# An mLSTM cell and a multiplicative feed-forward block on one core: first steps without products of zero states, other unread products, w_out fetched later

## The chip, the core and the metric

The kernel runs on one core of one Trainium2 chip. The metric is the device time in microseconds (us), from the start to the end of one execution. Lower is better. The kernel before has a median of 429.15 us over 3 runs (426.0 to 430.21).

## What is computed

The first half is an mLSTM cell over 4 sequences of 768 steps with 8 heads of 40 elements. Its output, seen as 3072 tokens of 320 elements, is the input of a feed-forward block in which two products are multiplied element by element:

```python
# per step t; C (40x40) and n (40) start at zero, m is a running maximum
m_new = np.maximum(f_gate[:, :, t] + m, i_gate[:, :, t])
f_stab = np.exp(f_gate[:, :, t] + m - m_new)
i_stab = np.exp(i_gate[:, :, t] - m_new)
C = f_stab * C + i_stab * np.einsum('bhd,bhe->bhde', vt, kt)
n = f_stab * n + i_stab * kt
h_tilde = np.einsum('bhde,bhe->bhd', C, qt)
denom = np.maximum(np.abs(np.einsum('bhd,bhd->bh', n, qt)), 1.0)
y[:, :, t] = sigmoid(o_gate) * h_tilde / denom
...
a = x @ w1          # 3072x320 @ 320x1024
b = x @ w2
h = a * b @ w3      # 1024x1024
return h @ w_out    # 1024x320
```

All data is float32.

## The kernel before

**Tiling.** The sequences are cut into 6 stretches of 128 steps, each of two chunks of 64. A unit is one stretch of one sequence with all heads: 24 units, n = 0 to 23, and unit n belongs to sequence n % 4. The main loop (L812) runs 32 steps s. Step s does the inner part of unit s (scores of q and k, and the new contribution to the state) and the output of unit s-1. The feed-forward products of finished units are put into the same steps, so that TensorE has work while the other engines prepare the next unit. w3 is multiplied into w_out on the chip (`w3_mm`, L256), so that only the product of both is used at the end.

**What a step's cell consists of (`quarter_work`, L335).** For unit s-1: 16 products `ph` of the masked weights pw with v, and 16 products `pi` of q with the state that the unit began with. For unit s: 16 products `ss` of k with q, and 16 products `pc` of k with weighted v, which VectorE adds to the state. Each of these is 64 wide at most, so four of them sit in the four quarters of the TensorE array, in the order of `quarters` (L104). In `pi`, hip is the half of the array's rows and x the chunk, that is the half of its columns; chunk x = 0 reads the state before the unit and x = 1 the state between the two chunks:

```python
for p in range(NP):
    for hip, x in quarters:            # quarters = ((0, 0), (1, 1), (0, 1), (1, 0))
        mm(pi[halves[x], hip, p, :], qT[heads[hip], p, halves[x]], before[x][heads[hip], p, :])
```

In the first four units the state before the unit is all zeros. The results of `ss` and `pc` are in the PSUM tile `cell0`, those of `pi` (and of `ph` from unit 2 on) in `cell1`.

**Order.** TensorE's instructions stay in the order in which they are written: `mm` (L91) and `transpose` (L94) chain each one to the one before (`in_order`, L84). Every `mm` of float32 appears in the trace as two weight loads (PEld) and two matmuls (PE), a transpose as one of each. On the other engines the order is the scheduler's; `keep_order` and `issue_after` hold parts of it. The queue of SyncE (SP) issues nearly all loads, in the order of the code.

**Products that nobody reads.** `warm(n)` (L97) multiplies the identity by itself n times into a spare PSUM bank. It is called with 8 at L579, before the first transposes, and with 5 at L893, in the function `between` of step 2, between `x_trans(0)` and `x_trans(1)`. `x_trans(n)` (L473) transposes the output y of unit n, as three transposes into a tile px, for the feed-forward block; it needs y of that unit from VectorE (L440).

**Step 2.** `between` (L884) scales and converts weight pieces, transposes y of units 0 and 1, turns unit 2's q and k (`turn`, tiles pt), and does the first feed-forward products (`up`, tiles pa and pb, and `up_rest` with the rest of the weights, wr).

**Weights.** The weights come as raw 8-byte words: `fetch` (L208) issues the DMA into one of the raw buffers, `scale_next` (L230) scales it on ScalarE (L188, L192), and `convert` (L234) makes float32 of it on VectorE (L196, L197). After the 10 pieces of w1, w2 and their rest come 8 of w_out and 16 of w3. `n_cvt[s]` (L806) pieces are converted at the end of step s. At the end of a step the loop at L968 fetches until `fetched` is 4 ahead of `converted`.

**PSUM.** Four banks (`ps_m`) serve the tiles of `mps` (L77) in turn; a bank can be written when its earlier tile has been read.

Of the kernel before, what the change touches and what calls it, by code (L numbers as in the profile page):

```python
# [16 lines left out]
def kernel(  # L17
# [26 lines left out]
    nc = tc.nc  # L44

    B, H, S, D = q.shape
    L = 64
    P = 128
# [3 lines left out]
    NP = H // 2  # L52
    DP = 64
    D1 = D + 1
# [20 lines left out]
    cell = [ps_c.tile([P, 2, 512], FP, name=f"cell{i}", tag=f"cell{i}") for i in range(2)]  # L75

    def mps(shape, name):  # L77
        pool = banks.pop(0)
        banks.append(pool)
        return pool.tile(shape, FP, name=name, tag="m")  # L80
# [3 lines left out]
    def in_order(ins):  # L84

        if last:
            tc.add_manual_dep(ins.ins, last.pop().name, mybir.DependencyInfo(
                mybir.DependencyClass.NoSync, mybir.DependencyReason.DATA), reason="in_order")
        last.append(ins.ins)

    def mm(out, lhsT, rhs, start=True, stop=True):  # L91
        in_order(nc.tensor.matmul(out, lhsT=lhsT, rhs=rhs, start=start, stop=stop))  # L92
# [1 line left out]
    def transpose(out, in_, n=P):  # L94
        in_order(nc.tensor.transpose(out, in_, ident[0:n, 0:n]))  # L95

    def warm(n):  # L97
        bank = mps([P, P], "fill")
        for _ in range(n):
            mm(bank, ident, ident)  # L100

    halves = [slice(0, L), slice(L, P)]
    heads = [slice(0, D), slice(DP, DP + D)]
    quarters = ((0, 0), (1, 1), (0, 1), (1, 0))  # L104
# [4 lines left out]
    N_DIAG = 2  # L109
# [5 lines left out]
    ident = const.tile([P, P], FP, name="ident")  # L115
# [179 lines left out]
    def weights(n):  # L295
        c, b = divmod(n, B)
        src = weights_tile(n) if n else spread(n)
        pw = weights_tile(n)
        for h in range(H):
            nc.scalar.activation(out=pw[:, h, :], in_=src[:, h, :], func=AF.Exp, bias=aT[:, c, b * H + h:b * H + h + 1])  # L300
# [7 lines left out]
    def turn(n):  # L308


        if n >= N_DVE:
            for src, dst, name in zip(turned_in[n % 2], (kT_t, qT_t), ("kT", "qT")):
                dst[n] = sb.tile([128, NP, P], FP, name=name, tag=name)
                done = nc.vector.transpose(out=dst[n].rearrange("i p (r f) -> i p f r", f=4),
                                           in_=src[:, 32:TB].rearrange("i (p f d) -> i p f d", p=NP, f=4)[:, :, :, 0:32])
            return done
        for src, dst, name in ((kbuf[n % NB], kT_t, "kT"), (qbuf[n % NBQ], qT_t, "qT")):
            pt = mps([128, NP, P], "pt")
            for p in range(NP):
                transpose(pt[:, p, :], src[:, 2 * p:2 * p + 2, :].rearrange("p a b -> p (a b)"))  # L320
            dst[n] = sb.tile([128, NP, P], FP, name=name, tag=name)
            nc.scalar.copy(out=dst[n], in_=pt)
# [12 lines left out]
    def quarter_work(s, rest, between, late):  # L335


        rest()

        def part(j, c0, n):  # L340
            return cell[j][:, :, c0:c0 + NP * n].rearrange("p x (n d) -> p x n d", d=n)

        ss, pc, pi = part(0, 0, L), part(0, NP * L, D1), part(1, 0, D1)
        ph = [cell[1][:, x, NP * D1:2 * NP * D1].rearrange("p (h d) -> p h d", d=D1) for x in range(2)]
        n = s - 1
        if 0 <= n < NU:
            pw, vt, qT = u_t.pop(n), vbuf[n % NBV], qT_t.pop(n)
            before = before_t.pop(n)

            if n < N_DIAG:  # L350
                ph = mps([P, H, D1], "ph")
                for hq in range(H):
                    for r in halves:
                        mm(ph[r, hq, :], pw[r, hq, :], vt[r, hq, :])
            for hd in range(H // 2 if n >= N_DIAG else 0):
                for x, e in quarters:
                    hq = hd if x == e else hd + H // 2
                    mm(ph[x][halves[e], hd, :], pw[halves[x], hq, :], vt[halves[x], hq, :])
            for p in range(NP):
                for hip, x in quarters:  # L360
                    mm(pi[halves[x], hip, p, :], qT[heads[hip], p, halves[x]], before[x][heads[hip], p, :])
        den = None
        if 0 <= s - 1 < NU:
            den = outputs(s - 1, pi, ph)
            den()
            if between:
                for _ in range(3):
                    den()
                den = None
                between()  # L370
            if late:
                late()
        n, first_read = s, None
        if n < NU:
            c, b = divmod(n, B)
            kt, vw = kbuf[n % NB], vw_t.pop(n)
            ends = range(2 if c < NT2 - 1 else 1)
            first, second, after = state[b]
            before_t[n] = first, second
            state[b] = after, second, first  # L380
            kT, qT, pw = kT_t.pop(n), qT_t[n], u_t[n]
            for p in range(NP):
                for hip, x in quarters:
                    mm(ss[halves[x], hip, p, :], kT[heads[hip], p, halves[x]], qT[heads[hip], p, halves[x]])
            M = D if n else L
            for p in range(NP):
                for x, e in quarters:
                    if x in ends:
                        mm(pc[e * L:e * L + M, x, p, :], kt[halves[x], 2 * p + e, 0:M], vw[halves[x], 2 * p + e, :])
        if n < NU:  # L390
            pv = pw.rearrange("p (n two) t -> p two n t", two=2)
            first_read = nc.vector.tensor_tensor(out=pv, in0=ss, in1=pv, op=OP.mult)
        with tc.issue_after(first_read.ins) if first_read else nullcontext():
            if den:
                den()
            if n < NU:

                if c:
                    nc.vector.tensor_tensor(out=second, in0=pc[:, 0], in1=second, op=OP.add)  # L399
                else:  # L400
                    nc.vector.tensor_copy(out=second, in_=pc[:, 0])
                if len(ends) > 1:
                    decayed(after, second, n, 1)
            if late:
                late()
            if den:
                den()
            if n < NU and len(ends) > 1:
                nc.vector.tensor_tensor(out=after, in0=pc[:, 1], in1=after, op=OP.add)
            if den:  # L410
                done = den()
        return done if den else first_read
# [104 lines left out]
    fetch("w12", 4, 0)  # L517

    nc.vector.memset(on, 1.0)
    nc.vector.memset(on.rearrange("p (c t) -> p c t", t=L)[:, :, 0:1], 0.0)  # L520
    nc.vector.memset(M[third[0], 0:1], 0.0)
    make_identity(nc, ident)
# [49 lines left out]
    def gate_cols(src, dst, copy):  # L572
        pg = mps([P, GC // 2, GR, BH], "pg")
        for c in range(GC // 2):
            transpose(pg[:, c].rearrange("p g r -> p (g r)"), src[:, c * P:(c + 1) * P], RG)
        for c in range(GC // 2):
            copy(out=dst.rearrange("p (g c) r -> p c g r", g=GR)[:, c], in_=pg[:, c])

    warm(8)  # L579
    turn(0)  # L580
    gate_cols(a, aT, nc.scalar.copy)
    nc.scalar.activation(out=dec, in_=U3[:, :, L - 1], func=AF.Exp)
    scale_next(True)
# [4 lines left out]
    for i, r in enumerate(third):  # L588
        nc.gpsimd.tensor_tensor(out=pick[r, :, i, :], in0=pair[r].to_broadcast([BH, B * NP, GC]), op=OP.mult,
                        in1=dec[r].unsqueeze(1).to_broadcast([BH, B * NP, GC]))  # L590
    weights(0)
    gate_cols(w, wT, nc.scalar.copy)
    weighted(0)
    masks(0)
# [208 lines left out]
    n_out = [0] * 27 + [1, 0, 1, 0, 3]  # L803
    w12 = [("w12", i, part) for part in range(2) for i in range(2 * KF + 1)]
    todo = w12[5:] + [("wo", i, 0) for i in range(FO)] + [("w3", ko, part) for ko in range(FO) for part in range(2)]
    n_cvt = [0, 0, 2, 0, 1, 2, 3, 3, 3] + [2] * 6  # L806
    n_fetch = [5, 5, 10]
    pinned, ahead = 32, 9
    behind = ExitStack()
    turned, converted, fetched = 0, 2, 5  # L810

    for s in range(len(n_up)):  # L812
# [4 lines left out]
        if s < 3:  # L817
# [6 lines left out]
            if s == 2:  # L824
                for _ in range(2):
                    fetch(*todo.pop(0))
                fetched = 10
# [56 lines left out]
        def between():  # L884
            twice(1)
            weighted(2)
            rows_of_u(3)
            for _ in range(3):
                scale_next()
            for n in range(2):  # L890
                x_trans(n)
                if n == 0:
                    warm(5)  # L893
            for _ in range(3):
                convert()
            turn(2)
            block = up(*now[0])
            weighted(3)
            weights(3)
            masks(3)  # L900
            out_gate(2)
            convert()
            up_rest(*block)
# [32 lines left out]
        if s in (2, 3):  # L936
            turned, converted = 2, converted + (4 if s == 2 else 2)
# [27 lines left out]
                scale_next()  # L965
        if N_DVE <= s + 2 < NU:
            load_turned(s + 2)
        while todo and fetched < (n_fetch[s] if s < len(n_fetch) else converted + 4):  # L968
            fetch(*todo.pop(0))
            fetched += 1  # L970
        if s + 1 == pinned:
# [32 lines left out]
```

## Time and profile before

| what | value |
|---|---|
| the profiled execution | 430.57 us |
| its span, first to last instruction | 428.5 us |
| three runs | 426.0, 429.15, 430.21 us |
| TensorE matmul busy / weight load busy | 410.7 us (96%) / 336.6 us (79%) |
| VectorE, ScalarE, GpSimd busy | 312.2, 149.8, 154.7 us |
| mean granted TensorE clock | 0.992 |
| moved by DMA | 51.15 MB, 135211 packets, mean 119 GB/s |
| instruction queue of TensorE (q8) | 42 packets, 0.69 MB |

A time in the views is counted from the start of the span. In a timeline a row gives the start, the length, the engine, the line of code, the operation, what it writes and reads, the shape (`64*64 64x41` is a weight tile of 64 rows and 64 columns and a result of 64 x 41) and the number of instructions. In brackets stands the idle time of the engine before it and what ended it; "issue" means that the engine waited for nothing that the profile shows. Most of `mm`'s calls have L92 as their line, so groups are told apart by their tiles.

### The profile page before, as it was taken

The numbers are of one execution on the slowest core, as the hardware profiler recorded it, in microseconds if no ns is written. First come the engines' busy times: TensorE is split into PE (matmuls) and PEld (weight loads), VectorE is DVE, ScalarE is ACT, GpSimd is POOL, SyncE is SP. The second block draws the span as 40 slices with busy tenths as digits, with TensorE's granted clock in tenths as the row PEclk, the third lists the DMA queues.
The fourth block names the chain that finished last, engine by engine and source line by source line (L and its number), as shares of the span: only waits on it lengthen the run. The fifth ranks groups of instructions, "written<-read, shape, count | busy, mean of one in ns | idle before, by whom it ended". The sixth has DMA issues, their size and how long they took to land.

```text
span 428.5 us, 13080 instructions
## 1 busy us (share of the span) xinstructions
PE 410.7 (96%) x5353; PEld 336.6 (79%) x5353; DVE 312.2 (73%) x634; ACT 149.8 (35%) x404; POOL 154.7 (36%) x211
## 2 busy tenths in 40 slices
PE   7789979999999999999999999999999999999996
PEld 5678768888788688788777677787778778888896
DVE  6768874788949769779726866586877699575972
ACT  4866843576725514521333313132311110210000
POOL 4530431333203113203307833645462577542200
PEclk9999969999999999999999999999999999999999
DMA  8999888398897866886335566666421120000001
GB/s 188 219 177 231 202 141 141 93 198 189 210 188 142 186 173 116 187 161 133 73 95 112 139 130 148 138 139 112 100 43 37 35 38 2 31 2 31 2 32 61
DMA packets 135211, 51.15 MB, mean 119 GB/s; under 512 B 109360, under 2 KB 126960, under 8 KB 135152
## 3 DMA queue, kind: packets, MB, share of 16 engines
q1 hardware_dynamic: 131552, 46.29, 53.2%
q10 hardware_dynamic: 3600, 4.03, 2.7%
q8 instruction: 42, 0.69, 0.7%
q14 instruction: 17, 0.14, 0.1%
HBM read 44.50 MB, written 5.80 MB: 117 GB/s over the span
## 4 chain that ended last, share of the span: by engine, by line
PE 69%; issue 9%; SPq 7%; DMA 5%; DVE 4%; POOL 3%; ACT 0%; DVEq 0%; POOLq 0%; ACTq 0%
PE cell L92 19%; PE pa L92 19%; PE pb L92 12%; PE o L92 8%; PE wp L92 6%; PE p L92 3%; SPq L136 3%; DMA raw<-in_moe_w_dram 3%; SPq L181 2%; DVE w3T L658 1%; PE pt L95 1%; POOL pw L305 1%; POOL raw L651 1%; PE px L95 1%; SPq L150 1%
## 5 line engine op out<-in xcount | busy, mean ns | idle before, releaser
L332 POOL TENSOR_TENSOR state<-state,decay 128x164 f32<-128x164 f32 x40 | 20.2, 504 | 154.7 <-DVE state L399 127.1
L92 PE MATMUL pa<-xT,w 128*128 128x256 f32 x240 | 62.0, 390 | 0.0
L92 PEld LDWEIGHTS pa<-xT,w 128*128 128x128 f32 x240 | 45.5, 195 | 6.8
L300 ACT ACTIVATE pw<-pw,aT 128x64 f32<-128x64 f32 x184 | 46.4, 337 | 3.2 <-ACT o_sb L733 1.9
L92 PE MATMUL pb<-xT,w 128*128 128x256 f32 x192 | 45.6, 380 | 0.7 <-DVE w L197 0.7
L92 PEld LDWEIGHTS pb<-xT,w 128*128 128x128 f32 x192 | 36.5, 191 | 6.1 <-DVE w L197 1.1
L721 POOL TENSOR_TENSOR ab<-ab,a_sb 128x512 f32<-128x512 f32 x22 | 29.4, 1357 | 32.0 <-DVE ab L676 32.0
L703 POOL TENSOR_TENSOR wo<-wo 128x512 f32<-128x512 f32 x22 | 27.5, 1270 | 31.5 <-DVE wo L678 31.5
L92 PE MATMUL pa<-xT,wr 64*64 64x256 f32 x384 | 37.0, 386 | 0.7 <-DVE wr L197 0.7
L92 PE MATMUL wp<-wo,w3T 128*128 128x320 f32 x128 | 35.9, 433 | 1.5 <-issue 1.1
L305 POOL TENSOR_SCALAR_AFFINE_SELECT pw<-pw 64x512 f32<-64x512 f32 x48 | 36.0, 750 | 3.1 <-ACT pw L300 1.4
L92 PE MATMUL pb<-xT,wr 64*64 64x256 f32 x384 | 36.4, 380 | 0.0
L92 PE MATMUL cell<-w3o,ab 128*128 128x320 f32 x128 | 35.4, 432 | 0.0
L630 ACT ACTIVATE a_sb<-pa 128x512 f32<-128x512 f32 x24 | 14.3, 596 | 60.3 <-PE pb L92 60.3
L631 DVE TENSOR_TENSOR ab<-pb,a_sb 128x512 f32<-128x512 f32 x24 | 16.4, 688 | 25.4 <-ACT a_sb L630 25.1
L92 PEld LDWEIGHTS wp<-wo,w3T 128*128 128x128 f32 x128 | 23.8, 190 | 10.9 <-issue 1.3
L92 PEld LDWEIGHTS cell<-w3o,ab 128*128 128x128 f32 x128 | 24.3, 190 | 9.5
L92 PEld LDWEIGHTS pa<-xT,wr 64*64 64x64 f32 x384 | 18.9, 132 | 15.6 <-issue 8.8
L425 DVE TENSOR_TENSOR h<-cell,h 64x164 f32<-64x164 f32 x88 | 28.7, 326 | 1.7
L678 DVE SCALAR_TENSOR_TENSOR a_sb<-pa,wo 128x512 f32<-128x512 f32 x12 | 8.3, 689 | 28.1 <-PE pa L92 28.1
L92 PE MATMUL po<-w3o,ab 128*128 128x320 f32 x96 | 26.4, 433 | 0.0
L92 PEld LDWEIGHTS po<-w3o,ab 128*128 128x128 f32 x96 | 18.1, 190 | 7.3
(179 smaller groups left out, 837.3 us busy)
## 6 DMA issues: line engine op xcount, KB each, us to landing
raw<-in_moe_w_dram SPq DMA_DIRECT2D x64, 128.0 KB, 3.2
kbuf<-in_k_dram SPq DMA_DIRECT2D x24, 160.0 KB, 4.4
v_all<-in_v_dram SPq DMA_DIRECT2D x24, 160.0 KB, 4.8
o_in<-in_o_gate_dram SPq DMA_DIRECT2D x24, 160.0 KB, 4.9
pw<-U_d SPq DMA_DIRECT2D x28, 128.0 KB, 3.6
raw<-in_moe_w_dram SPq DMA_DIRECT2D x5, 512.0 KB, 6.2
raw<-in_moe_w_out_dram SPq DMA_DIRECT2D x8, 320.0 KB, 4.6
gates<-in_k_dram SPq DMA_DIRECT2D x28, 80.0 KB, 3.3
```

Source lines behind the costliest of these rows:

```text
L92: in_order(nc.tensor.matmul(out, lhsT=lhsT, rhs=rhs, start=start, stop=stop))
L95: in_order(nc.tensor.transpose(out, in_, ident[0:n, 0:n]))
L136: nc.sync.dma_start(out=dst, in_=rows(src, n))
L181: nc.sync.dma_start(out=dst, in_=src)
L300: nc.scalar.activation(out=pw[:, h, :], in_=src[:, h, :], func=AF.Exp, bias=aT[:, c, b * H + h:b * H + h + 1])
L305: nc.gpsimd.affine_select(out=pw[r], in_=pw[r], compare_op=OP.is_ge, fill=0.0, base=0, pattern=[[0, H], [1, L]], channel_multiplier=-1)
L332: nc.gpsimd.tensor_tensor(out=new, in0=old, op=OP.mult, in1=decay[:, b * NP:(b + 1) * NP, 2 * c + x:2 * c + x + 1] .to_broadcast([P, NP, D1]))
L425: nc.vector.tensor_tensor(out=part, in0=ph[x][halves[e]], in1=part, op=OP.add)
L630: nc.scalar.mul(out=a_sb, in_=pa, mul=UP ** -2)
L631: nc.vector.tensor_tensor(out=ab_t[gr][j][:, fs[0]:fs[-1] + 1, t0:t0 + a_sb.shape[-1]], in0=pb, in1=a_sb, op=OP.mult)
L703: aside_by.tensor_tensor(out=kept[j][:, 1:4:2], in0=kept[j][:, 1:3], in1=kept[j][:, 3:4].to_broadcast([128, 2, TH]), op=OP.add)
L721: aside_by.tensor_tensor(out=t[:, f:FO:FH, :], in0=t[:, f:FO:FH, :], in1=a, op=OP.mult)
```

## The change

Five things are changed.

- In units 0 to 3 (n < B) only `quarters[1:3]`, that is (1, 1) and (0, 1), are multiplied in `pi`: 8 products instead of 16. The place of the 8 that are left out is set to zero once, by a memset on VectorE.
- `warm` gets a width: m copies of c columns of the identity.
- The unread products: 2 of 512 columns instead of 8 of 128 at the start; one of 256 columns before each of the first two `gate_cols`; one of 512 columns before `ph` in steps 1 and 2.
- Between `x_trans(0)` and `x_trans(1)` 39 unread products of 8 columns stand in place of 5 of 128. Both programs then have 2742 matmuls and transposes on TensorE: 32 are taken out of `pi`, the 13 unread ones become 45.
- w_out: at the end of steps 3 and 4 the loop fetches up to 2 and 3 pieces ahead of the conversion instead of 4, and the conversion of one piece moves from step 4 to step 7.

In the built program the loads of w_out at the end of steps 3, 4, 5 and 6 are 2, 1, 3 and 2 instead of 4, 1, 2 and 1; the instructions on TensorE, apart from those listed, are the same in the same order.

```diff
-    def warm(n):
-        bank = mps([P, P], "fill")
+    def warm(n, m=4, c=P):
+        bank = mps([P, 4, P], "fill")
         for _ in range(n):
-            mm(bank, ident, ident)
+            mm(bank[:, 0:m, 0:c], ident, ident[:, 0:c].unsqueeze(1).to_broadcast([P, m, c]))
...
             before = before_t.pop(n)
+            if n < N_DIAG:
+                warm(1)
...
-                for hip, x in quarters:
+                for hip, x in quarters if n >= B else quarters[1:3]:
                     mm(pi[halves[x], hip, p, :], qT[heads[hip], p, halves[x]], before[x][heads[hip], p, :])
...
     nc.vector.memset(on, 1.0)
+    nc.vector.memset(cell[1][halves[0], :, 0:NP * D1], 0.0)
...
-    warm(8)
+    warm(2)
     turn(0)
+    warm(1, 2)
     gate_cols(a, aT, nc.scalar.copy)
...
     weights(0)
+    warm(1, 2)
     gate_cols(w, wT, nc.scalar.copy)
...
-    n_cvt = [0, 0, 2, 0, 1, 2, 3, 3, 3] + [2] * 6
+    n_cvt = [0, 0, 2, 0, 0, 2, 3, 4, 3] + [2] * 6
...
             for n in range(2):
                 x_trans(n)
                 if n == 0:
-                    warm(5)
+                    warm(39, 1, 8)
...
-        while todo and fetched < (n_fetch[s] if s < len(n_fetch) else converted + 4):
+        while todo and fetched < (n_fetch[s] if s < len(n_fetch) else converted + min(s - 1, 4)):
```

## The prediction

> **What bounds the kernel now.** First the page's busy times and clock, then TensorE by stretch, then the timelines around the places that change.
>
> ```profile
> PE 410.7 (96%) x5353; PEld 336.6 (79%) x5353; DVE 312.2 (73%) x634; ACT 149.8 (35%) x404; POOL 154.7 (36%) x211
> ...
> PEclk9999969999999999999999999999999999999999
> ```
>
> TensorE is busy 96% of the span, and one slice, the sixth (54 to 64 us), has a lowered clock. The windows say where the rest is (columns: length, busy us of PE, PEld, DVE, ACT, POOL, clock, DMA share, GB/s):
>
> ```profile
> 25.30:42.50 17.20, 17.17 (x293) 14.66 (x293) 12.29 (x27) 10.66 (x24) 3.55 (x6) 1.00 1.00 224
> 42.50:46.50 4.00, 2.68 (x37) 1.88 (x38) 3.83 (x9) 3.13 (x9) 1.43 (x2) 1.00 0.69 94
> 46.50:55.67 9.17, 9.17 (x290) 8.06 (x278) 7.90 (x20) 7.04 (x22) 4.64 (x9) 1.00 1.07 234
> 55.67:58.26 2.59, 0.00 (x1) 0.00 (x1) 2.41 (x6) 0.00 (x0) 0.49 (x2) 0.88 0.79 120
> 58.26:64.50 6.24, 6.24 (x33) 5.47 (x34) 3.99 (x12) 4.17 (x13) 1.93 (x4) 0.50 0.80 144
> 64.50:428.50 364.00, 358.21 (x4346) 291.70 (x4344) 264.00 (x517) 107.75 (x288) 131.40 (x151) 1.00 0.50 106
> ```
>
> From 25.3 us on TensorE has three holes: 1.3 us at 42.5 to 45.4 (two waits of 0.66 for converted weights, L197), 2.59 us at 55.67, and 5.8 us spread over the last 364, its end included. So what delays TensorE after 25 us is paid at the end, less what these holes take up.
>
> The hole at 55.67 ends with "issue": the engine waits for nothing shown. It is the arrival of instructions. Queue q8 moved 42 packets of 16.4 KB for 10,706 loads and matmuls, about 255 a packet. Counted down the timeline, three "issue" holes (20.75, 55.67, 145.92 us) stand before matmuls 345, 976 and 2243: 631 and 1267 apart, 5 and 10 packets. In the trace the packet before the second one ran from 55.13 to 56.63; TensorE went on 1.63 us later. The previous boundary was crossed at 53.24, so a block that is worked off in under 5.0 us waits. After it comes half clock, 58.26 to 64.5: 3.1 us more. The place costs 5.7 us in this execution. The runs' spread (426.0 to 430.21) is as large as that half clock, so I take it that some runs lack it.
>
> The place of the 39 products:
>
> ```profile
> 21.87 0.48 PE L92 MATMUL cell<-state,qT 40*64 40x41 f32 x17 [1.12 <-issue]
> 22.28 0.55 PE L95 MATMUL px<-ident,y 128*128 128x128 f32 x3
> 22.66 1.28 PE L92 MATMUL fill<-ident 128*128 128x128 f32 x10
> 25.33 0.54 PE L95 MATMUL px<-ident,y 128*128 128x128 f32 x3 [1.39 <-DVE y L440]
> ```
>
> Five unread products take 1.28 us of a wait for y of unit 1 that lasts 2.67 us. How fast loads of 128 columns can follow each other shows where two start on an idle array:
>
> ```profile
> 43.20 0.19 PEld L92 LDWEIGHTS pb<-xT,w 128*128 128x128 f32 x1 [1.06 <-DVE w L197]
> ```
>
> ```profile
> 43.31 0.19 PEld L92 LDWEIGHTS pb<-xT,w 128*128 128x128 f32 x1
> ```
>
> They start 0.109 us apart.
>
> **What the Trainium skill says.** "TensorE: Matmul & The Clock Gate", LDWEIGHTS: a load takes its columns / 1.2 GHz, whatever the rows: 107 ns for 128. The trace agrees (109). The same page, Part 1: the clock halves after a window of about 3.4 us that counts as idle. The trace agrees in length (the half clock lasts 6.83 us, two windows), and shows that part of a window is enough: 1.46 us busy of 3.41 lost the clock, 2.02 kept it. Part 3 says that products in different parts of the array run together; the trace agrees below. "Runtime: NRT & Kernel Launch", Instruction fetch mechanics, says that instructions come in blocks of 256 and that the cost is "mostly hidden"; the block agrees, the hiding fails in the three holes.
>
> **The change, part by part.**
>
> *Products of zero states.* 32 of 64 go. Four quarters work at once: `pi` is 32 matmuls in 0.47 us (54.32 to 54.79), 8 in each quarter, 0.059 us apart. What goes is two of the four quarters, so the other two still need 8 x 0.059 = 0.47. Gain 0; at most half, 4 x 0.23 = 0.9, if same-column quarters had been sharing. I take 0. The memset (about 0.3 us by the 0.27 of its neighbour at L519) falls ahead of a 0.75 us wait of VectorE for the gates.
>
> *Fills of 512 and 256 columns.* At the start, 4 long matmuls for 16 short ones: equal columns. 512 columns are 0.86 us by the pace of 0.216 per 256-column matmul; they fit the waits of 1.15 and 1.23 us before `ph` (15.75, 19.39). 256 columns are 0.43: before the first pg there are 0.35 us, but ScalarE reads it only after 7.90; before the second, 0.70. Together 0, at worst 0.3, which the wait for y covers.
>
> *The 39 products.* Each is two loads of 128 columns and two matmuls of 8. A load cannot be much faster than 0.109, whatever the matmul does: `ph`, with 41 columns on 64-column loads, runs at the loads' pace (0.95 us for 15 loads in each of two quarters, 0.063). So 78 x 0.109 = 8.5 us (9.4 at the 0.120 of the fill's own loads). px 1 then starts at 22.66 + 8.5 = 31.2 instead of 25.33: 5.8 us late, up to 6.7. The "issue" hole at 20.75 disappears in it (matmul 345 falls into the tiny products), which makes y of unit 1 at most 0.3 us earlier; that no longer matters. Queued behind are the rest of TensorE's work, and by way of it xT, kT, qT (ScalarE), ab, h and the conversions behind them (VectorE).
>
> *What the later holes give back.* The first conversion (w, 42.46 to 43.15) follows ab and h of step 3 on VectorE; followed through, it is ready near 48.0 and TensorE arrives at 48.3: this 0.66 is gone. The second (wr) follows pw: ready near 50.2, TensorE at 50.0: about 0.3 remains. So 1.0 of 5.8 comes back: 4.8 late. Ends: 4.5 and 6.7.
>
> *w_out later.* Step 3 issues two loads of 320 KB fewer, about 3 us of DMA at 220 GB/s, and step 4 converts one piece less (1.2 us of VectorE that TensorE doesn't wait for). w_out is wanted by `w3_mm` at 110 us, and its conversion still ends in step 7 (85 to 95 us): hidden. The effect wanted is on the packet at 55. But the block boundary now comes at 58.0, and SP, with two loads less in front, will by then have the loads of unit 7 in flight, as it had those of unit 6 before: the queue is as full. I take 0.3 us off the 2.59 (ends 0 and 1.6) and the half clock as staying (ends 0 and 3.1).
>
> Sum: 4.8 - 0.3 = 4.5. Span 428.5 + 4.5 = 433.0, the execution 430.57 + 4.5 = 435.1; it lay 1.4 above the median of the runs, so 433.7 us.
>
> **The rivals.**
>
> *A: the tiny products lose the clock.* With 8 columns a matmul streams 7 ns of each 109. If the clock's monitor counts that as idle, half clock begins 3.4 to 6.8 us after 22.66, the remaining loads take double (2 to 4 us more), and the way back costs 2.5 more: 4.8 + 6 = 10.8 late. The later boundary then meets an empty DMA queue (1.3 us and often the 3.1 less). 429.15 + 10.8 - 2.8 = 437. For it: the reason for the lost clock at 57.6 is part of a window. Against: TensorE is never without an instruction here.
>
> *B: the packet at 55 comes early.* With a calm queue blocks arrived 3.5 to 3.9 us after the boundary, (95.36 to 98.82; 143.3 to 147.0), so the hole is 1.1 to 1.5 instead of 2.59, and the clock stays: -1.3 -3.1. 429.15 + 4.8 - 4.4 = 429.6. For it: the two loads were landing at 53.7 and 54.7. Against: 58.0 meets unit 7's loads.
>
> *C: not slower: repeated loads are cheap.* If a load and matmul of the tiny kind take under 2.67 / 78 = 0.034 us, all 39 are hidden in the wait for y, and with B's gain 429.15 - 4.4 = 424.8 comes out; above 0.034 each 10 ns cost 0.8 us. Against: the fill itself loads the same identity again and again, at 0.120.
>
> **How the numbers follow.** Forecast 40% (433.7, own range 432 to 436.5), A 32%, B 20%, C 8%. The range from 429.3 to 440.0 leaves out C, and the ends of A and B. A measurement of this kernel can tell about 1% (4.3 us) from no change. Slower by over 1% (over 433.4): A and six tenths of the forecast, with the ends of B and C's threshold, 0.63. Within 1%: B, four tenths of the forecast, half of C: 0.31. Faster: 0.06.
>
> **What would show it.** The fill group before px 1 should hold 78 matmuls and last 8.5 us, px 1 start near 31, and the wr products of step 4 near 50.2 instead of 45.43. `cell<-state` in steps 1 to 4 should show 16 matmuls in the same 0.47 us. The "issue" hole at 20.75 should be gone, and one stand near 60.5 before matmul 976. Loads at 0.055 or less, px 1 before 27, or a hole at 42 to 50 that takes up more than 1.5 us would make the forecast wrong; a clock of 0.50 inside the fill means A.

## The result, and the profile after

The changed kernel takes 438.41 us in the median of 4 runs (437.72 to 440.39), the kernel before 428.44 (4 runs): a ratio of 1.0255, 95% interval 1.0206 to 1.0304. That is 10.0 us slower, where 4.5 were forecast. The time lies inside the range on record, the direction is the forecast one, but the size is that of rival A. The profiled execution took 440.39 us, its span is 438.6.

The page of the changed kernel, busy times and clock by slices of 11 us:

```profile
PE 426.8 (97%) x5353; PEld 349.7 (80%) x5353; DVE 312.6 (71%) x635; ACT 149.5 (34%) x404; POOL 154.8 (35%) x211
...
PEclk9955999999999999999999999999999999999999
```

The same 5353 matmuls keep TensorE busy 16.1 us longer than before (426.8 against 410.7), and the weight loads 13.1. VectorE, ScalarE and GpSimd have what they had. The lowered clock has moved from the sixth slice to the third and fourth. The timeline of TensorE there:

```profile
21.74 0.71 PE L95 MATMUL px<-ident,y 128*128 128x128 f32 x3 [1.13 <-DVE y L442]
22.28 15.95 PE L92 MATMUL fill<-ident 128*128 128x8 f32 x78
38.09 0.88 PE L95 MATMUL px<-ident,y 128*128 128x128 f32 x3
```

The 78 matmuls of the 39 products take 15.95 us where 8.5 were forecast. px of unit 1 starts at 38.09, 12.8 us later than before (25.33). The windows show why (columns: length, busy us of PE, PEld, DVE, ACT, POOL, clock, DMA share, GB/s):

```profile
22.28:38.09 15.81, 15.81 (x80) 15.81 (x79) 5.90 (x13) 2.23 (x5) 1.67 (x3) 0.52 1.03 227
38.09:43.52 5.43, 5.43 (x20) 4.80 (x21) 0.00 (x0) 3.88 (x13) 0.24 (x1) 0.50 1.23 165
43.52:70.00 26.48, 25.85 (x553) 21.93 (x551) 20.77 (x48) 16.20 (x40) 8.34 (x15) 1.00 0.71 124
70.00:71.10 1.10, 0.00 (x0) 0.00 (x0) 1.04 (x4) 0.00 (x0) 0.00 (x0) 1.00 0.00 0
71.10:128.50 57.40, 56.98 (x859) 47.34 (x859) 46.81 (x103) 37.21 (x96) 16.68 (x30) 1.00 0.74 157
```

TensorE is busy in every microsecond of the first two stretches, and its clock is 0.52 and 0.50 in them: by the trace's record of the clock, half clock stands from 23.05 to 43.52 us, 20.5 us or six windows of 3.41. The last 5.4 us of it fall on real work. Then the clock stays at 1.00 for the rest.

Two later places of the changed kernel's timeline answer to the hole at 55.67 of before, and show a wait that before doesn't have:

```profile
71.11 0.35 PE L92 MATMUL cell<-vw,kbuf 64*40 64x41 f32 x12 [1.21 <-issue]
...
129.61 1.56 PE L92 MATMUL pa<-xT,w 128*128 128x256 f32 x6 [1.06 <-ACT xT L483]
```

How much later each matmul starts than its twin in the kernel before, read from both timelines:

| place (time in the kernel after) | late by, us | what happened since the row above |
|---|---|---|
| px of unit 1 (38.09) | 12.8 | 78 tiny matmuls at half clock |
| end of half clock (43.5) | 15.4 | 5.4 us of px, pt and pa at half clock |
| after the wr products (59.7) | 14.2 | one of the two waits for weights is gone |
| after the hole (71.1) | 12.8 | hole of 1.21 instead of 2.59 |
| where before has its half clock (74.4) | 9.9 | the clock stays at 1.00 here |
| after the wait for xT (129.6) | 10.5 | a wait of 1.06 |
| end | 10.1 | small holes |

### The profile page after: what moved, and what is told of

It is laid out like the page before. It is cut to its first block, busy times and chain, and to the rows that moved or that the text cites. A ratio compares the mean times of both kernels' runs of the same rounds, so it can differ in the third digit from the quotient of the medians.

```text
span 438.6 us, 13080 instructions
## 1 busy us (share of the span) xinstructions
PE 426.8 (97%) x5353; PEld 349.7 (80%) x5353; DVE 312.6 (71%) x635; ACT 149.5 (34%) x404; POOL 154.8 (35%) x211
## 4 chain that ended last, share of the span: by engine, by line
PE 75%; DVE 10%; DMA 6%; issue 3%; ACT 3%; SPq 2%; POOL 0%; DVEq 0%; ACTq 0%; POOLq 0%
PE cell L92 19%; PE pa L92 17%; PE pb L92 11%; PE o L92 8%; PE wp L92 6%; PE po L92 4%; PE fill L92 4%; PE p L92 3%; DMA raw<-in_moe_w_dram 3%; PE px L95 1%; DVE w3T L663 1%; SPq L181 1%; ACT pw L300 1%; PE pt L95 1%; DVE h L427 1%
## 5 line engine op out<-in xcount | busy, mean ns | idle before, releaser
L92 PE MATMUL fill<-ident 128*128 128x8 f32 (+2 forms) x90 | 23.2, 398 | 1.6 <-POOL ident masks.py:199 1.6
```

## The experiments

All times are medians, and each ratio is to the kernel before (427.5 to 428.1 in these runs) with its 95% interval; a ratio is not the quotient of the two medians and differs from it by up to 0.4%. An edit of the changed kernel leaves everything else of the change in place. No kernel leaves out a product that the output depends on: what the zero states' edit leaves out multiplies zeros.

### Is it the number of loads, or the clock?

Theory: the tiny products lose the clock, because they stream too little, and that doubles the time of their loads and of what follows. Rival: loads that follow each other simply take longer than 0.109 us, whatever the clock. Two kernels keep the 78 loads of 128 columns and change only how many columns each matmul streams:

```diff
-                    warm(39, 1, 8)
+                    warm(39, 1, 128)      # e2_wide_products
+                    warm(39, 1, 32)       # e8_quarter_wide_products
```

On record for 128 columns: 

> The changed kernel, with the 39 unread products 128 columns wide instead of 8 (16 times the streaming, same loads). If the loads set the pace and the lack of streaming cost the clock, the group takes 78 x 0.111 = 8.7 us at a clock of 1.00, although it does 16 times the work, px 1 starts near 31 us, and the kernel takes about 432 to 434 us, 5 to 7 less than the changed kernel. Rival: the length comes from the number of small instructions, and the clock from something else (the wait of 1.1 us in front): then the group takes as long as in the changed kernel or longer, 16 us or more, and the time is 438 or more.

On record for 32 columns: 

> The changed kernel with 39 products of 32 columns: 27 ns of streaming in each 109 ns of load, a quarter, against 6% with 8 columns and all with 128. If the clock's monitor counts streaming and its bound lies above a quarter, the group takes 15 to 16 us at half clock and the time is 437 to 440, as in the changed kernel; if it lies below, the group takes 8.5 to 8.7 us at full clock and the time is 432 to 434.

Measured: 432.84 us with 128 columns (1.0105, 1.0068 to 1.0142), 439.89 with 32 (1.0238, 1.0204 to 1.0272). The fill and px of unit 1 in the timeline of the 128-column kernel:

```profile
23.20 8.87 PE L92 MATMUL fill<-ident 128*128 128x128 f32 x78
31.91 0.49 PE L95 MATMUL px<-ident,y 128*128 128x128 f32 x3
```

and in that of the 32-column kernel:

```profile
22.95 16.14 PE L92 MATMUL fill<-ident 128*128 128x32 f32 x78
38.90 0.88 PE L95 MATMUL px<-ident,y 128*128 128x128 f32 x3
```

With the same number of loads the fill takes 8.87 us or 16.14. The windows over the two fills, first 128 columns, then 32 (columns as above, the clock stands before the last two):

```profile
23.20:31.90 8.70, 8.70 (x79) 8.70 (x79) 6.02 (x13) 2.85 (x6) 1.71 (x3) 1.00 1.00 184
```

```profile
23.55:44.03 20.48, 20.48 (x92) 19.94 (x92) 5.38 (x11) 5.49 (x16) 1.68 (x3) 0.50 1.08 216
```

TensorE is busy without a break in both; only the streaming differs, and with it the clock. The rival falls.

Another rival is the wait of 1.13 us for y, which lies in the window in which the changed kernel loses its clock. The kernel before has a window with a hole as long (1.12 us, "issue") and as much busy time, and keeps it; its windows are counted back in steps of 3.41 us from 57.62, where its clock changes. First that one, then the changed kernel's (length, busy us of PE, clock, DMA share, GB/s):

```profile
20.07:23.49 3.42, 2.30 (x59) 1.00 1.26 132
```

```profile
19.63:23.05 3.42, 2.29 (x45) 1.00 1.07 131
```

The first ends with products of 128 columns and the clock stays, the second with tiny ones and the clock goes. So the wait and the busy time do not decide it; the kernel with narrow loads below even lost the clock after a window that was 2.42 us busy (20.16 to 23.57), and the kernel before kept it after one of 2.02 (23.49 to 26.90). That narrow products take the clock from a window without any wait is not shown: in all five kernels that lost it during such a fill, that window held a wait too. What they do by themselves is keep it from coming back: four windows of 3.41 us hold nothing else, with 8 columns (23.05 to 36.70) and with 32 (23.55 to 37.20), and half clock follows each.

A load and its matmul take 8.87 / 78 = 0.114 us at full clock. A matmul of 256 columns comes every 0.216 us (eight from 72.64 to 74.37 us in the changed kernel), so one of 128 streams for 0.108 of that (95%), one of 32 for 0.027 (24%), one of 8 for 0.007 (6%).

A third kernel asks where between 24% and 95% the bound lies, with 64 columns (47%; the expectation counts 128 columns as 100%):

```diff
-                    warm(39, 1, 8)
+                    warm(39, 1, 64)       # e9_half_wide_64
```

On record: 

> The changed kernel with the 39 products 64 columns wide: the same 78 loads of 128 columns[...]. With 24% (32 columns) the clock was halved for 20.5 us and the kernel took 439.9; with 100% (128 columns) it stayed at 1.00 and the kernel took 432.8. If the monitor asks for less than half of the time in streaming, this one keeps the clock: the fill lasts 8.5 to 8.9 us and the time is 432 to 434. If it asks for more than half, half clock stands from about 23.5 to 44 and the time is 438 to 441. Between the two: the clock is lost in some windows of the fill and not in others, 434 to 438.

Measured: 435.57 us in the median of six executions. Its timeline, and the windows over its fill:

```profile
22.98 8.82 PE L92 MATMUL fill<-ident 128*128 128x64 f32 x78
31.64 0.50 PE L95 MATMUL px<-ident,y 128*128 128x128 f32 x3
```

```profile
22.98:31.80 8.82, 8.82 (x81) 8.82 (x81) 5.87 (x13) 2.72 (x6) 1.81 (x3) 1.00 0.99 178
```

In this execution 47% kept the clock. Four of the six executions took 433.89 to 435.71, 434.8 in their median (1.0158, 1.0123 to 1.0192), with a mean clock of 0.992 to 0.995. The other two took 441.0 and 441.1 with a mean clock of 0.977, the changed kernel's own. That fits a bound that this kernel sometimes misses, but those two executions have no trace. The 434.8 is 0.8 above the expected 432 to 434; the profile has the hole before matmul 977 (976 in the kernel before, whose trace has one record less ahead of it) and the half clock after it, which the 128-column kernel lacks:

```profile
63.31 0.50 PE L92 MATMUL cell<-vw,kbuf 64*40 64x41 f32 x12 [2.57 <-issue]
63.75 0.90 PE L95 MATMUL px<-ident,y 128*128 128x128 f32 x3
```

### Is the width of the loads what sets the length?

The changed kernel with the 39 products on 32 columns of the identity as weights, so that a load has 32 columns instead of 128:

```diff
+    def narrow(n, k, c):
+        bank = mps([P, 4, P], "fill")
+        for _ in range(n):
+            mm(bank[0:k, 0, 0:c], ident[:, 0:k], ident[:, 0:c])
...
-                    warm(39, 1, 8)
+                    narrow(39, 32, 8)     # e1_narrow_loads
```

On record: 

> The changed kernel, with the 39 unread products loading 32 columns of the identity instead of 128 (results 32 x 8 instead of 128 x 8, same number of instructions). If the width of the load sets their length, 78 loads and matmuls take 0.025 to 0.04 us each, 2 to 3 us in all, px 1 starts at 25 to 26 us as before the change, and the kernel takes about 425 to 430 us: 10 to 13 us less than the changed kernel. Rival: a matmul of 8 columns waits for its own load and drain, whatever the load's width, so the group stays at 0.2 us each, 15 us or more, and the time at 438. Whether the clock still steps down during the group says what its monitor counts: with 2 to 3 us at a low share, a step is possible but not sure.

Measured: 430.61 us (1.0061, 1.0027 to 1.0095). Its timeline:

```profile
22.64 3.72 PE L92 MATMUL fill<-ident 128*32 128x8 f32 x78
26.30 0.90 PE L95 MATMUL px<-ident,y 128*128 128x128 f32 x3
```

3.72 us instead of 15.95, so the loads' columns set the length. The clock is lost here as well (half clock from 23.57 to 30.39), but for two windows instead of six, as the fill is over sooner. The time is 0.6 above the 425 to 430 on record; the profile has a longer hole later (2.86 us before matmul 977).

### Are the 39 products the whole loss?

The kernel before with only the 39 products (e3), and the changed kernel with only them undone (e4):

```diff
-                    warm(5)               # e3_tiny_alone, in the kernel before
+                    narrow(39, P, 8)
...
-                    warm(39, 1, 8)        # e4_five_again, in the kernel after
+                    warm(5, 1)
```

On record for the products alone: 

> The kernel before, with only the 5 unread products between the two transposes of y replaced by the 39 of 8 columns (the program gets 34 products longer, so the blocks of instructions fall elsewhere from there on). If they alone make the change slow, the group takes 14 to 16 us at half clock and the time is 8 to 13 us above the kernel before, 436 to 441. If the extra time needs another part of the change (the zero states, the later w_out), it is within 3 us of the kernel before.

On record for all but the products: 

> The changed kernel, with 5 unread products of 128 columns instead of the 39 of 8 (34 products shorter, the blocks of instructions fall elsewhere). The rest of the change then stands alone. By the theory that the 39 products are the whole loss, 425 to 430 us, at or below the kernel before. Rival: the other parts, or the places of the block boundaries, cost time too: 431 or more, with an issue hole of more than 2 us somewhere before 110 us.

Measured: 441.17 us (1.0286, 1.0248 to 1.0323) with the 39 alone, 430.40 (1.006, 1.0031 to 1.0089) without them. In the kernel with the 39 alone:

```profile
24.86 16.07 PE L92 MATMUL fill<-ident 128*128 128x8 f32 x78
40.78 0.88 PE L95 MATMUL px<-ident,y 128*128 128x128 f32 x3
```

So the products cost 13 us by themselves, just above the 8 to 13 on record, and 8.0 (438.4 - 430.4) beside the rest. Not all of the 13 need be theirs: the profile of the kernel with the 39 alone also has half clock from 8.43 to 18.67 us, ahead of them, and reaches the fill 2.2 us later than the kernel before (24.86 and 22.66). The rest of the change costs 2.5 of its own, where the forecast had a gain of 0.3; so the theory that the 39 are the whole loss fails by that much. The timeline of the kernel without the 39 has a wait that before does not have:

```profile
117.57 1.99 PE L92 MATMUL pa<-xT,w 128*128 128x256 f32 x8 [3.07 <-ACT xT L483]
```

### What does w_out later do?

The kernel before with the two lines of w_out's schedule alone (e5). Then the narrow loads (e1) and the five products (e4) once more, each with before's schedule of w_out (e7, e10):

```diff
# e5_w_out_alone, in the kernel before; e7 and e10 undo the same two lines
-    n_cvt = [0, 0, 2, 0, 1, 2, 3, 3, 3] + [2] * 6
+    n_cvt = [0, 0, 2, 0, 0, 2, 3, 4, 3] + [2] * 6
...
-        while todo and fetched < (n_fetch[s] if s < len(n_fetch) else converted + 4):
+        while todo and fetched < (n_fetch[s] if s < len(n_fetch) else converted + min(s - 1, 4)):
```

On record for w_out alone: 

> The kernel before, with only w_out fetched and converted later. By the forecast's step the hole before matmul 976 keeps 2.3 to 2.6 us and the rest is hidden: 427 to 428.5. Rival from the changed kernel's profile: the hole is 1.2 us and the clock stays (4.4 us less there), but the pieces of w3 come later, ScalarE's scaling of them holds up the copy to xT behind it, and a new wait of 1 to 3 us stands before pa near 117 us: 425 to 427.

On record for the narrow loads with w_out early: 

> The changed kernel with loads of 32 columns in the 39 products, and with w_out fetched and converted as before the change. Beside the run with the later w_out (430.61 us): if the later w_out costs the wait before pa near 119 us (1.68 us there) and gives nothing back, this one is 1 to 2 us faster, 428.5 to 430, and its wait near 119 is under 0.5 us. Rival: the later w_out helps the packet of instructions, then this one has a longer hole before matmul 976 and takes 431 to 433.

On record for the five products with w_out early: 

> The changed kernel with five products of 128 columns in place of the 39, and with w_out's words called for as in the kernel before: what is left of the change are the new fills and the products of zero states. With w_out later the same kernel took 430.4, the products of zero states alone took 426.4. If w_out later costs some 3 us as soon as the boundary of blocks has moved away from 55 (as it did beside the narrow loads: 430.6 against 427.4), this one takes 426 to 428 and the wait before pa at 117 us is gone or under 1 us. If the new fills are what costs, it stays at 429.5 to 431 and px of unit 1 or the first steps are later than with the old fills.

Measured, each beside its twin:

| | w_out as before | w_out later |
|---|---|---|
| the kernel before | 1 | 0.9995 (0.9974 to 1.0015), 427.68 us |
| narrow loads | 0.9981 (0.9959 to 1.0003), 427.44 us | 1.0061 (1.0027 to 1.0095), 430.61 us |
| five products | 1.0007 (0.9989 to 1.0024), 428.14 us | 1.006 (1.0031 to 1.0089), 430.40 us |

Alone it is worth nothing; beside the rest it costs 3.2 and 2.3 us. The narrow loads with w_out early are 1 us below the 428.5 to 430 on record, and have no wait near 116 us. The two effects of w_out later stand in the timeline of the kernel with w_out later alone:

```profile
56.45 0.35 PE L92 MATMUL cell<-vw,kbuf 64*40 64x41 f32 x13 [1.49 <-issue]
...
116.79 1.99 PE L92 MATMUL pa<-xT,w 128*128 128x256 f32 x8 [1.35 <-ACT xT L481]
```

The hole before matmul 976 is 1.49 instead of 2.59, and the half clock after it lasts one window instead of two. At 117 us a wait for xT takes 1.35 back. Where it comes from: ScalarE, in its order, scales pieces of w3 as they land, and copies px to xT behind the fourth of them. In the kernel with five products and w_out later (the 3.07 above):

```profile
113.74 0.69 ACT L188 ACTIVATE raw<-raw 128x512 f32<-128x512 f32 x1 [1.05 <-DMA raw<-in_moe_w_dram]
114.31 0.65 ACT L192 ACTIVATE raw<-raw 128x512 uint32<-128x512 uint32 x1
115.94 0.68 ACT L188 ACTIVATE raw<-raw 128x512 f32<-128x512 f32 x1 [0.98 <-DMA raw<-in_moe_w_dram]
116.51 0.65 ACT L192 ACTIVATE raw<-raw 128x512 uint32<-128x512 uint32 x1
117.06 0.46 ACT L483 COPY xT<-px 128x384 f32<-128x384 f32 x1
```

ScalarE waits for DMA, px waits behind, and TensorE for xT. With w_out later, w3's words are called later too, since they stand behind w_out's in the same list. SP's queue in this kernel, and then in its twin with w_out early, at the end of the same step:

```profile
77.85 1.74 SPq L181 DMA_DIRECT2D raw<-in_moe_w_dram  x4
87.10 8.57 SPq L181 DMA_DIRECT2D raw<-in_moe_w_dram  x16
```

```profile
78.26 3.76 SPq L181 DMA_DIRECT2D raw<-in_moe_w_dram  x8
```

Four transfers of w3 instead of eight; the other four come 9 us later. Across this place, from matmul 1735 to 1838, the kernels fall behind the kernel before by 3.4 us with w_out later and 1.6 with w_out early (five products), by 1.3 and 0.4 (narrow loads). For the narrow loads the wait so explains 0.9 us of the 3.2. For the five products it explains less than the 1.8 that the two numbers differ by: with w_out later that kernel was 1.3 us earlier at matmul 1735 (103.66 against 104.93) and waited these away, and its copy to xT came 0.5 us later (117.06 against 116.53). Of its 2.3 us the two profiles show only 0.6 at the end, so most of it stays open. The wait is also there without w_out later where TensorE comes early: the five products with w_out early kept one of 1.28 us and came to 428.14, just above the expected 426 to 428.

For the narrow loads the rest stands at the boundary of blocks. With w_out later, and then with w_out early:

```profile
60.30 0.35 PE L92 MATMUL cell<-vw,kbuf 64*40 64x41 f32 x12 [2.86 <-issue]
```

```profile
58.16 0.35 PE L92 MATMUL cell<-vw,kbuf 64*40 64x41 f32 x12 [0.45 <-issue]
```

Here the hole is longer with w_out later, where alone it was shorter. What the holes follow is the packet of instructions: in the DMA records of the traces, queue q8 has one that ends ahead of each hole's end.

| kernel | the packet on q8, us | next matmul starts | hole before it |
|---|---|---|---|
| before | 55.13 to 56.63 | 58.26 | 2.59 |
| w_out later alone | 53.74 to 55.10 | 56.45 | 1.49 |
| narrow loads, w_out later | 57.81 to 58.75 | 60.30 | 2.86 |
| narrow loads, w_out early | 55.21 to 56.75 | 58.16 | 0.45 |
| 64 columns | 60.34 to 61.92 | 63.31 | 2.57 |
| 128 columns | 56.81 to 58.45 | 60.80 | none |
| after | 68.40 to 69.83 | 71.11 | 1.21 |

In all 14 traces there are 42 "issue" holes of over 0.15 us on TensorE, and each ends 1.25 to 1.82 us after a packet on q8 has ended. So a hole is as long as TensorE comes ahead of that moment. What makes one packet run later than another is not shown, and w_out's schedule alone does not settle it.

### Do the products of zero states gain anything?

The kernel before with only them left out (e6):

```diff
-                for hip, x in quarters:
+                for hip, x in quarters if n >= B else quarters[1:3]:
...
+    nc.vector.memset(cell[1][halves[0], :, 0:NP * D1], 0.0)
```

On record: 

> The kernel before, without the 32 products of zero states (and with the memset), nothing else. Two quarters of the array instead of four: the 16 matmuls take the same 0.47 us, so no time by themselves. The program is 32 products shorter, a block boundary falls 128 instructions elsewhere, and the holes that wait for instructions move: 426 to 431 by that alone. A gain of the products themselves would show as 0.2 us less in each of the four steps.

Measured: 426.43 us, 0.6% less than before (0.9937, 0.991 to 0.9965), the fastest of all. The products themselves give next to nothing: the cell's four groups (`ph`, `pi`, `ss`, `pc`), from their first matmul to the transposes behind them, take 1.81 us in steps 3 and 4 for 1.92 and 1.82 before. In the timeline of this kernel half of them in step 2, and all of them in step 5, take the same time:

```profile
20.16 0.67 PE L92 MATMUL cell<-state,qT 40*64 40x41 f32 x15
...
54.34 0.66 PE L92 MATMUL cell<-state,qT 40*64 40x41 f32 x32
54.81 0.67 PE L92 MATMUL cell<-qT,kT 40*64 40x64 f32 x32
55.30 0.49 PE L92 MATMUL cell<-vw,kbuf 64*40 64x41 f32 x32
```

But the group of 32 at 55.30 is whole: no "issue" hole at this place. 64 matmuls fewer have moved the boundary of blocks. Two kernels put the old numbers back, by unread products of 32 columns on 32-column loads: 40 of them in place of the first fill (e11), or eight in each of steps 1 to 4, where the products of zeros had stood (e12):

```diff
-    warm(8)
+    narrow(40, 32, 32)                    # e11_zero_states_same_length
...
+            if n < B:
+                narrow(8, 32, 32)         # e12_zero_states_replaced
```

On record for the first: 

> The kernel before with the products of zero states left out (they multiply states that are zero) and the first fill made of 40 products of 32 columns on 32-column loads instead of 8 of 128, so that from step 4 on every matmul has its old number again. The products alone without this took 426.4, 0.6% less than before, and had no hole near 55 us. If that gain came from the boundary of blocks moving away from 55 us, the hole before matmul 976 is back here (1.2 to 2.6 us) and the time is 427.5 to 430, no difference to before. If the gain came from the products themselves, the time stays at 425.5 to 427 with the hole there or not. If the first fill takes longer than the 3.8 us of the old one, the start of the first transposes after it shows it, and that comes on top.

On record for the second: 

> The kernel before with the eight products of zero states in each of steps 1 to 4 left out (they multiply states that are zero) and eight small unread ones (32 columns on 32-column loads) in their place: the work on zeros is gone, every matmul keeps its number and its time of day, so the boundaries of blocks lie where they lay before. Left out alone, the products gave 0.6% (426.4). If that gain came from the boundaries having moved, it is gone here: 427 to 429, and the hole before matmul 976 stands again at 54 to 57 us, 1.2 to 2.6 us long. If it came from the work left out, the time is 426 to 427 in spite of the hole.

Measured: 428.15 us (1.0003, 0.9982 to 1.0025) and 427.51 (1.0004, 0.9978 to 1.0029). In both the gain is gone. The first one settles nothing by that: its extra products come so early that TensorE runs into a boundary of blocks it then waits at, in its timeline

```profile
23.53 0.23 PE L92 MATMUL cell<-vw,kbuf 64*40 64x41 f32 x1 [5.30 <-issue]
...
60.99 0.35 PE L92 MATMUL cell<-vw,kbuf 64*40 64x41 f32 x13 [0.94 <-issue]
```

and px of unit 1 is 5.1 us late; it ends level with before because the hole before matmul 976 is 0.94 and no half clock follows. The second one has the old numbers, and its median is the one expected if the boundary is the cause. But its matmuls are not at the old times: the products put in take time of their own, so that the cell's groups of steps 3 and 4 last 2.58 us each for 1.92 and 1.82 before, 1.4 us more in all. And its profiled execution (span 424.2) shows no hole there:

```profile
56.71 0.67 PE L92 MATMUL cell<-qT,kT 40*64 40x64 f32 x32
57.20 0.49 PE L92 MATMUL cell<-vw,kbuf 64*40 64x41 f32 x32
```

So it settles nothing either: 1.4 us of added work is nearly the 1.7 us by which the medians had come down (428.1 to 426.4). What is shown is that the work left out gives at most 0.1 us a step, and that the profile of the kernel without it lacks the hole of 2.59 us and the half clock behind it. That the boundary's place gives the 0.6% is likely by this, and not shown.

## Why the prediction was wrong in size

*The 39 products* is the step that failed. It set the length as 78 x 0.109 = 8.5 us, full clock taken. The runs show that this sum is right where the clock stays: 8.87 us with 128 columns, px of unit 1 at 31.91 for the forecast 31.2, and 432.84 us in all, 4.9 above before for the forecast 4.5. (The total agrees partly by luck: that kernel has lost its 6.6 us again by 65 us, because the hole and the half clock of before are missing, and falls behind by a wait of 2.77 for xT at 120 us and one window of half clock after it.) What is wrong is the argument for the clock, "TensorE is never without an instruction here". It is never without one, and the clock goes all the same. The term measured 15.95 us. By the medians, the 10.5 us between the kernel before of these runs (427.9) and the changed one divide as follows: 5.6 the clock (438.4 - 432.8), 2.4 the length of the fill at full clock (432.8 - 430.4), 2.5 the rest of the change (430.4 - 427.9). Each of the three is net of what the later holes of its two kernels took or gave back.

*Rival A* had the mechanism and, at 437, nearly the time. Two of its sizes were off. It let half clock begin 3.4 to 6.8 us after the fill's start; it began after 0.8 us, since the window that ended there, from 19.64 on, held the wait of 1.13 us for y and 0.8 us of tiny matmuls. So nearly all loads ran at half clock, and px was 12.8 late instead of 8 to 10. And it let 2.8 come back at the later boundary; from 15.4 down to 10.1, 5.3 came back. The two misses have opposite signs, so that its 437 came so near is in part luck. Its reason for the shorter hole fits: DMA was idle there (0.00 in the row 70.00:71.10). "The Trainium skill", page "TensorE: Matmul & The Clock Gate", Part 1, says that the monitor halves the clock after an idle window and that the windows run freely, without regard to the kernel. The traces agree with the windows: half clock comes in multiples of 3.41 us, and the first change of the clock on record stands anywhere from 4.57 to 7.46 us in the 14 traces. They show more than the page's idle: after a window in which the engine always works, but streams a quarter of the time or less, half clock goes on. The mark was there to be seen before: the trace of the kernel before had lost its clock after a window that was 1.46 us busy, and I read "busy" as the engine's records have it.

*What the later holes give back* was right in kind: the first of the two waits is gone, the second is 0.53 for a forecast 0.3. The 128-column kernel, nearly as late there as forecast, has 0.51, and its wr products start at 50.77 for the forecast 50.2.

*w_out later* failed in two points. The hole was to shrink by 0.3 and the half clock to stay; in the changed kernel it shrank by 1.4 and the half clock went. With the clock kept in the fill, the 64-column kernel shows what I had forecast, in place and size: a hole at 60.74 us, 2.57 long, and half clock after it. In the profile it ends 5.1 us after before, and the median of its four executions is 7.0 above. The 128-column kernel starts the same group of matmuls at 60.61 and runs through it without a hole, although TensorE works off the block ahead of this boundary in 2.2 us (58.58 to 60.80); so the forecast's mark, a block done in under 5.0 us waits, does not hold. Its packet had ended at 58.45, that of the 64-column kernel at 61.92. Which of the two an execution gets is open. The second point is the cost: I called the later w_out hidden, because its own use is late. What it delays is w3 behind it in the list. Beside the rest of the change that comes to 2.3 to 3.2 us, of which the wait for xT is 0.5 to 0.9.

*Products of zero states* were worth 0 in TensorE's time, as forecast: 16 matmuls take the 0.67 us of 32. *Fills of 512 and 256 columns*: px of unit 0 starts at 21.74 for 22.28 before, so they cost nothing there; the five products with w_out early, where fills and zero states are what is left, come to 1.0007.

*Rival B* had the smaller hole and the kept clock; both happened at 71 us, but in a kernel 14 us late. *Rival C* is refuted: the loads cost 0.114 us each at full clock.

A version that beats both kernels is the kernel before without the products of zero states, 426.43 us, and without anything put in their place; its lead on the kernel before is 0.6%.

## What to carry to other kernels

Work that is put in to keep TensorE's clock up must stream columns: count columns streamed per load, not whether the engine has an instruction. When a filler keeps a program's length, price it at half clock as well as at full, and price the real work that runs until the clock is back. When a transfer is moved back in a list, ask what stands behind it in that list, and which engine's order ties that to the critical one.

## What the runs showed of the hardware

- Half clock without one idle microsecond: with fills at 6% and 24% of the time in streaming the clock stayed at 0.50 for six windows (20.48 us each, four of them the fill alone), at 95% it stayed at 1.00; at 47% it was kept in the traced execution. Busy time does not tell: of two windows that were 2.30 and 2.29 us busy the first kept the clock.
- The way back takes part of the next real work: after the last tiny matmul at 38.09 another 5.4 us ran at 0.50.
- Weight loads slow with the clock: with 128 columns they start 0.112 us apart at 1.00 (128-column kernel) and 0.213 at 0.50 (changed kernel, 23.1 to 38.2 us). "The Trainium skill", page "TensorE: Matmul & The Clock Gate", LDWEIGHTS, gives columns / 1.2 GHz, 0.107 us, which holds at full clock alone.
- An "issue" hole at a boundary of instruction blocks was anything from nothing to 5.30 us long, the longest where 80 short matmuls had brought TensorE to the boundary early. All 42 of over 0.15 us in the 14 traces ended 1.25 to 1.82 us after a packet of the instruction queue had ended.
